# Hash attention and a squared-ReLU MLP on one core: the first pair's query hash products, score halves and first weight piece are put in other places

## The chip, the cores and the metric

The kernel runs on 1 core of one Trainium2 chip, in one launch. The metric is the device time of the kernel in microseconds (us). Before the change the median of 3 runs is 877.55 us (877.53 to 877.87).

## What is computed

Four batches of eight heads with 768 positions of 64 features: queries and keys are hashed to 6 bits by the signs of a projection, attention is allowed only between equal hashes, and the result, (4, 768, 8 x 64) seen as 3072 rows of 512, goes through a two-matrix MLP with a squared ReLU. The weights arrive as 64-bit floats.

```python
q_bucket = np.sum((np.einsum('bhsd,dk->bhsk', q, proj) > 0) * powers, axis=-1)   # k_bucket alike
mask = q_bucket[:, :, :, None] == k_bucket[:, :, None, :]
scores = np.where(mask, scale * np.matmul(q, k.transpose(0, 1, 3, 2)), -1e9)
attn = np.exp(scores - np.max(scores, axis=-1, keepdims=True))
attn = attn / (np.sum(attn, axis=-1, keepdims=True) + 1e-09)
x = np.matmul(attn, v)                     # then (B,H,S,D) -> (B*S, H*D)
r = np.maximum(x @ w_in, 0.0);  out = (r * r) @ w_out
```

## The kernel before, in words

**Stages.** The first stage (to about 330 us of the span) is attention, in a Python loop over 16 pairs of heads, `for pr in range(NP)`. The second is the MLP, with its matrices cut into factors (sums of blocks) so that fewer products are needed; the change does not touch it. Everything is emitted under a manual schedule: each engine executes its instructions in the order in which the code names them.

**One pair.** The two heads of a pair lie on the two halves of the 128 partitions. `feat[pr, w]` holds queries (w = 0) or keys (w = 1) with the features on the partitions. `hash_bits` (matmuls of L346) multiplies them by `projs`; the signs become `bits`, on ScalarE (`signs`, L356) or, for the first pair's keys, on VectorE (`first_keys`, L370 and L374). `score(pr, kt)` makes the scores of one block of 128 keys against all 768 queries: a bf16 product of the bits (the mask) and an fp32 product of the features are added up in one PSUM tile, and ScalarE's exponential (L413) writes them to `e`, one of a ring of four. The 768 queries are cut by `CUTS` into 512 and 256, with one PSUM tile for each cut. `add_up` (L423, L428, VectorE) adds the `e` to `total`; `attend` (L438) multiplies them by the values. Six blocks kt make a pair.

**What one pair leaves to the next.** `finish(pr - 1)`, called within pair pr behind `score(pr, 1)`, issues on TensorE, in this order: the hash products of pair pr + 1 (L346), which need `features(pr + 1)` (two transposes on VectorE, L333); the products `tot` with ones (L455), which need `total`; the last two `attend`; and `spread` (L477), which needs `both`, VectorE's L460, L462 and L466 behind `tot`. `normalize` writes `x_t`.

**PSUM tiles.** `turn()` hands out three tiles in turn, for transposes, hash products, scores and `tot` alike. A matmul that starts a new use waits until the reader of the use three turns before is done.

**The first pair** has its own start: q, k and `projs` are loaded from SP's and ScalarE's queues; TensorE transposes q and k (`first_features`, L309), in two rounds of three blocks of 128 positions each, and ScalarE (L316, q) or VectorE (L318, k) copies them out of PSUM. `keep_busy` (L326) issues matmuls without a use while the loads are under way. The feature products of `score(0, 0)` are issued ahead of its bit products.

**The weights.** They are loaded in 32 pieces of 128 x 512 64-bit floats, two in each pair (a = 2 pr, b = 2 pr + 1), and rounded to fp32 by hand: `part_weight` (VectorE, L143 and L147) splits the exponent from the high word, `place_power` (ScalarE, L160 and L161) moves it to its place, `round_weight` (VectorE, L171, L176, L179) puts sign, mantissa and exponent together and frees the raw piece (one of three buffers), and, for the last piece of each half only, sends DMAs. Piece a is rounded in its own pair and piece b in the next, but for pair 0: there the order of the code is that `place_power(0)` stands behind all six scores and `weigh(1)` (L382, the next pair's keys' bits times their weight), and `round_weight(0)` in pair 1, behind `features(2)`.

Of the kernel before, what the change touches and what calls it, by code (L numbers as in the profile page):

```python
# [34 lines left out]
def kernel(  # L35
# [13 lines left out]
    B, H, S, D = q.shape  # L49
# [5 lines left out]
    HS = S // 2  # L55
# [5 lines left out]
    CUTS = (0, 512), (512, S)  # L61
# [42 lines left out]
    def turn(name):  # L104

        return ps_s.tile([P, 2, 512], FP32, name=name, tag="turn")
# [11 lines left out]
    def goal(i):  # L118
        if i < 2 * NIN:
            return ins[i // NIN][:, i % NIN // 2, i % 2]  # L120
        return p_t.tile([P, DM], FP32, name="out_piece", bufs=3)
# [31 lines left out]
    def place_power(i):  # L153


        if i not in parts:
            return
        power = parts[i][0]
        small = p_w.tile([P, PIECE], U8, name="small")
        nc.scalar.activation(out=small, in_=power, func=ACTF.Relu, bias=excess)  # L160
        nc.scalar.activation(out=power, in_=small, func=ACTF.Copy, scale=2.0**23)  # L161

    def round_weight(i):

        raw = raws.pop(i, None)
        if raw is None:
            return keep_weight(i)
        goals[i] = goal(i)
        low, high = raw[:, :, 0], raw[:, :, 1]
        power, top = parts.pop(i)  # L170
        nc.vector.scalar_tensor_tensor(  # L171
            out=power, in0=high, scalar=0x80000000, in1=power,
            op0=ALU.bitwise_and, op1=ALU.bitwise_or,
        )
        one = top.bitcast(FP32)
        nc.vector.scalar_tensor_tensor(  # L176
            out=one, in0=low, scalar=2.0**-32, in1=top, op0=ALU.mult, op1=ALU.add,
        )
        nc.vector.scalar_tensor_tensor(  # L179
            out=goals[i], in0=one, scalar=2.0**-20, in1=power.bitcast(FP32),  # L180
            op0=ALU.mult, op1=ALU.mult,
        )
        keep_weight(i)

    def keep_weight(i):

        t = goals.pop(i)
        j, c = divmod(i, NIN)
        if j >= 2:
            nc.sync.dma_start(out=w_out_1[:, i - 2 * NIN], in_=t)  # L190
        elif c == NIN - 1:
            nf = NFT // 2
            for n, f, h in (0, 0, 0), (1, nf, 0), (2, nf, 1):
                put_factor(n, j * PIECE, ins[j][:, f:f + nf, h])
            nc.sync.dma_start(
                out=w_in_21[:, :, j * PIECE:(j + 1) * PIECE], in_=ins[j][:, 0:nf, 1]
            )
# [104 lines left out]
    def first_features(w, r):  # L302

        if r == 0:
            feat[0, w] = p_f.tile([P, S], FP32, name=f"feat{w}")
        tp = turn("tp")[:, 0]
        for i in range(SB // 2):
            t = r * (SB // 2) + i
            nc.tensor.transpose(  # L309
                out=tp[:, i * P:(i + 1) * P],  # L310
                in_=nat[0, ("q_nat", "k_nat")[w]][:, t].rearrange("p h d -> p (h d)"),
                identity=ident,
            )
        out = feat[0, w][:, r * HS:(r + 1) * HS]
        if w == 0:
            nc.scalar.copy(out=out, in_=tp[:, 0:HS])  # L316
        else:
            nc.vector.tensor_copy(out=out, in_=tp[:, 0:HS])  # L318

    busy = const.tile([P, 512], BF16, name="busy")  # L320
    void = ps_o.tile([P, 1024], FP32, name="xo")

    def keep_busy(n, w=512):

        for _ in range(n):
            nc.tensor.matmul(  # L326
                out=void[:, 0:w], lhsT=busy[:, 0:P], rhs=busy[:, 0:w], start=True, stop=True
            )
# [8 lines left out]
    def hash_bits(pr, banks, ws=(0, 1), cs=(0, 1)):  # L337


        for w in ws:  # L340
            hashed[pr, w] = banks
            for c in cs:
                g = 2 * w + c
                for h in range(2):
                    rows = slice(h * D, (h + 1) * D)
                    nc.tensor.matmul(  # L346
                        out=banks[g * NR_B:(g + 1) * NR_B, h, 0:HS], lhsT=projs[rows],
                        rhs=feat[pr, w][rows, c * HS:(c + 1) * HS], start=True, stop=True,
                    )

    def signs(pr, w):
        bits[pr, w] = t = all_bits[pr % 2][w]
        for c in range(2):
            at = slice((2 * w + c) * NR_B, (2 * w + c + 1) * NR_B)
            for h in range(2):
                nc.scalar.activation(  # L356
                    out=t[h * D:h * D + NR_B, c * HS:(c + 1) * HS], in_=hashed[pr, w][at, h, 0:HS],
                    func=ACTF.Sign, scale=HUGE, bias=lifts[at],
                )
# [19 lines left out]
    def weigh(pr):  # L379

        t = bits[pr, 1]
        nc.scalar.activation(out=t, in_=t, func=ACTF.Copy, scale=gains)  # L382
# [3 lines left out]
    def score(pr, kt):  # L386

        e = ring[len(weights) % NRING]
        weights[pr, kt] = e
        key = slice(kt * P, (kt + 1) * P)  # L390
        sts = []

        def products(st, lo, hi, src, first):
            for h in range(2):
                rows = slice(h * D, (h + 1) * D)
                nc.tensor.matmul(  # L396
                    out=st[:, h, 0:hi - lo], lhsT=src[pr, 1][rows, key],
                    rhs=src[pr, 0][rows, lo:hi], start=first, stop=not first,
                )


        if (pr, kt) == (0, 0):
            for lo, hi in CUTS:
                sts.append(turn("st"))
                products(sts[-1], lo, hi, feat, True)
        for i, (lo, hi) in enumerate(CUTS):
            if len(sts) <= i:
                sts.append(turn("st"))
                products(sts[i], lo, hi, bits, True)
                products(sts[i], lo, hi, feat, False)  # L410
            else:
                products(sts[i], lo, hi, bits, False)
            nc.scalar.activation(  # L413
                out=e[:, :, lo:hi], in_=sts[i][:, :, 0:hi - lo], func=ACTF.Exp, scale=scale
            )
# [176 lines left out]
    with tc.manual_schedule():  # L592
# [10 lines left out]
        first_features(0, 0)  # L603
        first_features(0, 1)
        keep_busy(2)
        first_features(1, 0)
        hash_bits(0, void.rearrange("p (h c) -> p h c", h=2), (0,))
        signs(0, 0)
        first_keys(0, turn("hash"))
        first_features(1, 1)  # L610
# [3 lines left out]
        for pr in range(NP):  # L614
            a, b = 2 * pr, 2 * pr + 1
            more = pr + 1 < NP

            def prepare():

                hash_bits(pr + 1, turn("hash"))  # L620
                for w in (1, 0):
                    signs(pr + 1, w)


            if pr + 2 < NP:
                load_pair(pr + 2)
            if pr == X_0:
                load_x(0)
            if more and pr > 0:
                for w in range(2):  # L630
                    features(pr + 1, w)
            if pr > 0:
                if pr == 1:
                    round_weight(0)
                round_weight(b - 2)
                load_weight(b)
                for m in sums.get(pr, ()):
                    sum_in(m)
            score(pr, 0)
            if pr == 0:  # L640
                first_keys(1, turn("hash"))
            score(pr, 1)
            if pr == 0:
                for w in range(2):
                    features(1, w)
            if pr > 0:
                finish(pr - 1, prepare if more else None)
            add_up(pr, 1)
            if pr > 0:
                normalize(pr - 1)  # L650


            if pr == X_0 + 1:
                for n in range(2):
                    load_unit(n)
            part_weight(a)
            score(pr, 2)
            if pr == 0:
                prepare()
            score(pr, 3)  # L660
            if more and pr > 0:
                weigh(pr + 1)
            if pr > 0:
                place_power(a)
            attend(pr, 0)
            attend(pr, 1)
            for kt in (2, 3):
                add_up(pr, kt)
            if more:
                load_values(pr + 1)  # L670


            if pr > 0:
                round_weight(a)
            part_weight(b)
            if more:
                load_weight(a + 2)
            score(pr, 4)
            score(pr, 5)
            if pr == 0:  # L680
                weigh(1)
                place_power(0)
            place_power(b)
            attend(pr, 2)
            attend(pr, 3)
            add_up(pr, 4)
            add_up(pr, 5)
# [801 lines left out]
```

## Time and profile before

| what | value |
|---|---|
| median of 3 runs | 877.55 us |
| time of the profiled execution | 877.55 us |
| its span, first to last instruction | 875.8 us |
| what lies around the span | 1.75 us |
| TensorE busy | 864.5 us, 99% of the span |
| VectorE busy | 760.1 us, 87% |
| ScalarE busy | 391.7 us, 45% |
| mean granted TensorE clock | 0.997 |
| idle TensorE, 0 to 7 us / 7 to 12 / 12 to 21 / 21 to 36 | 1.48 / 0.00 / 0.27 / 0.74 us |
| idle TensorE, 36 to 56 / 56 to 320 / 320 to the end | 0.00 / 0.00 / 8.77 us |
| VectorE busy, 36 to 56 / 56 to 320 | 19.59 of 20.00 / 254.27 of 264.00 us |

A row of the timeline gives the start of a group of like instructions on one engine in us from the span's start, the time from its first start to its last end, the engine (PE is TensorE, PEld its weight loads, DVE VectorE, ACT ScalarE, SP and ACTq queues that issue DMAs), the line of the code, the operation, the tiles it writes and reads, the shape, the count, and in brackets how long the engine was idle before it and who ended that. Instructions of one engine overlap at their ends, so the next one can start a tenth of a microsecond before the row's end. An fp32 matmul shows as two records.

### The profile page before, as it was taken

How to read it: one execution, taken by the hardware profiler on the slowest of the kernel's cores; microseconds unless marked ns; L12 is line 12 of the kernel's file. 1: busy time of each engine (PE TensorE's matmuls, PEld its weight loads, DVE VectorE, ACT ScalarE, POOL GpSimd, SP SyncE). 2: the span in 40 equal slices, each digit the busy share in tenths (PEclk: the TensorE clock that was granted, in tenths of full speed). 3: DMA queues.
4: the chain of work that ended last, by engine and by line, in shares of the span. 5: the costliest groups of instructions: out<-in, count | busy, mean ns of one | idle time of the engine just before them, and what ended most of it. 6: DMA issues, size and time to landing. Idle time of an engine off the chain costs nothing.

```text
span 875.8 us, 12135 instructions
## 1 busy us (share of the span) xinstructions
PE 864.5 (99%) x4340; PEld 519.3 (59%) x4340; DVE 760.1 (87%) x1099; ACT 391.7 (45%) x673; POOL 107.1 (12%) x172
## 2 busy tenths in 40 slices
PE   8999999999999999999999999999999999999996
PEld 4444444444444444444688865556888755568885
DVE  5999999999999998888689978888889788888875
ACT  6988788888888852222211123332111233321110
POOL 2000000000000001554032111112000211110002
PEclk9999999999999999999999999999999999999998
DMA  9787967999879526999787874536756754355565
GB/s 176 146 154 134 232 156 150 194 244 234 179 172 226 164 98 223 294 263 288 299 291 259 219 172 156 173 125 219 282 161 177 166 169 152 124 169 158 154 171 109
DMA packets 224131, 167.09 MB, mean 191 GB/s; under 512 B 164448, under 2 KB 181344, under 8 KB 224064
## 3 DMA queue, kind: packets, MB, share of 16 engines
q1 hardware_dynamic: 189152, 87.19, 41.7%
q0 software_dynamic: 12528, 41.30, 15.2%
q10 hardware_dynamic: 22384, 37.76, 14.3%
q8 instruction: 36, 0.59, 0.3%
q14 instruction: 31, 0.25, 0.1%
HBM read 124.52 MB, written 41.68 MB: 190 GB/s over the span
## 4 chain that ended last, share of the span: by engine, by line
PE 95%; DVE 2%; SPq 1%; DMA 1%; issue 0%; ACT 0%; DVEq 0%
PE acc L717 40%; PE st L396 17%; PE acc L936 16%; PE xo L438 13%; PE acc L889 6%; PE hash L346 1%; PE tot L455 1%; DVE total L428 1%; DMA q_nat<-in_q_dram 1%; SPq L287 1%; PE xo L326 0%; PE tp L309 0%; DVE power L171 0%; DVE top L176 0%; DVE feat L333 0%
## 5 line engine op out<-in xcount | busy, mean ns | idle before, releaser
L413 ACT ACTIVATE e<-st 128x1024 f32<-128x1024 f32 x192 | 144.9, 810 | 44.4 <-PE st L396 40.7
L396 PE MATMUL st<-feat,feat 64*128 64x512 f32 (+1 forms) x768 | 150.4, 483 | 0.0
L438 PE MATMUL xo<-e,v_nat 128*64 128x512 f32 (+1 forms) x768 | 134.8, 492 | 0.0
L717 PE MATMUL acc<-b,leaf 128*128 128x256 f32 x600 | 133.1, 379 | 0.0
L717 PEld LDWEIGHTS acc<-b,leaf 128*128 128x128 f32 x600 | 113.8, 190 | 16.2 <-issue 0.9
L428 DVE TENSOR_TENSOR total<-total,e 128x1536 f32<-128x1536 f32 x64 | 112.4, 1756 | 8.1 <-ACT e L413 3.6
L438 PEld LDWEIGHTS xo<-e,v_nat 128*64 128x64 f32 x768 | 51.3, 136 | 82.2 <-issue 74.0
L936 PE MATMUL acc<-t_x,w_unit 128*128 128x512 f32 x192 | 90.2, 592 | 0.0
L396 PEld LDWEIGHTS st<-feat,feat 64*128 64x128 f32 x768 | 66.0, 188 | 32.4 <-issue 22.6
L717 PE MATMUL acc<-t,leaf 128*128 128x256 f32 x336 | 76.2, 380 | 0.0
L356 ACT ACTIVATE bits<-hash,lifts 32x384 bf16<-32x384 f32 x120 | 68.7, 573 | 1.9
L717 PEld LDWEIGHTS acc<-t,leaf 128*128 128x128 f32 x336 | 63.7, 190 | 9.1 <-DVE t L516 0.5
L801 DVE SCALAR_TENSOR_TENSOR b<-h 128x512 f32<-128x512 f32 x96 | 65.7, 692 | 3.0
L396 PE MATMUL st<-bits,bits 64*128 64x256 bf16 (+1 forms) x384 | 63.0, 325 | 0.7 <-ACT bits L356 0.5
L936 PE MATMUL acc<-x,w_unit 128*128 128x512 f32 x128 | 60.1, 592 | 0.0
L717 PE MATMUL acc<-x,w_unit 128*128 128x512 f32 x128 | 56.5, 593 | 0.0
L717 PE MATMUL acc<-b_t,leaf 128*128 128x256 f32 x240 | 53.8, 379 | 0.0
L936 PEld LDWEIGHTS acc<-t_x,w_unit 128*128 128x128 f32 x192 | 36.5, 190 | 28.8 <-issue 26.8
L724 ACT COPY two<-acc 128x256 f32<-128x256 f32 (+1 forms) x29 | 12.5, 432 | 87.7 <-PE acc L717 69.1
L724 ACT COPY one<-acc 128x256 f32<-128x256 f32 (+1 forms) x29 | 12.5, 432 | 84.3 <-PE acc L717 55.5
L717 PEld LDWEIGHTS acc<-b_t,leaf 128*128 128x128 f32 x240 | 45.5, 190 | 6.2
L396 PEld LDWEIGHTS <-bits 64*128 64x128 bf16 x384 | 23.6, 93 | 41.9 <-issue 37.7
(159 smaller groups left out, 1166.5 us busy)
## 6 DMA issues: line engine op xcount, KB each, us to landing
leaf<-w_out ACTq DMA_DIRECT2D x142, 256.0 KB, 3.2
w_unit<-w_in SPq DMA_DIRECT2D x16, 640.0 KB, 4.0
raw<-in_moe_w_in_dram SPq DMA_DIRECT2D x16, 512.0 KB, 5.5
raw<-in_moe_w_out_dram SPq DMA_DIRECT2D x16, 512.0 KB, 4.5
w_unit<-w_in SPq DMA_DIRECT2D x8, 896.0 KB, 7.8
w_out<-sums POOLq DMA_DIRECT2D x16, 448.0 KB, 6.8
sum<-w_in SPq DMA_DIRECT2D x16, 448.0 KB, 4.8
v_nat<-in_v_dram SPq DMA_DIRECT2D x16, 384.0 KB, 4.6
```

The costliest lines, as they stand in the source:

```text
L287: nc.sync.dma_start(out=t[g * 32:(g + 1) * 32].rearrange("i (c d) -> i c d", d=32), in_=src[b, 2 * j + h].rearrange("(c i) (e d) -> e i c ...
L346: nc.tensor.matmul(out=banks[g * NR_B:(g + 1) * NR_B, h, 0:HS], lhsT=projs[rows], rhs=feat[pr, w][rows, c * HS:(c + 1) * HS], start=True, ...
L356: nc.scalar.activation(out=t[h * D:h * D + NR_B, c * HS:(c + 1) * HS], in_=hashed[pr, w][at, h, 0:HS], func=ACTF.Sign, scale=HUGE, bias=li ...
L396: nc.tensor.matmul(out=st[:, h, 0:hi - lo], lhsT=src[pr, 1][rows, key], rhs=src[pr, 0][rows, lo:hi], start=first, stop=not first,)
L413: nc.scalar.activation(out=e[:, :, lo:hi], in_=sts[i][:, :, 0:hi - lo], func=ACTF.Exp, scale=scale)
L428: nc.vector.tensor_tensor(out=totals[pr], in0=totals[pr], in1=weights[pr, kt][:, :, 0:S], op=ALU.add)
L438: nc.tensor.matmul(out=xo[h * D:(h + 1) * D, lo:hi], lhsT=nat[pr, "v_nat"][:, h, kt * D:(kt + 1) * D], rhs=weights[pr, kt][:, h, lo:hi], s ...
L717: nc.tensor.matmul(out=acc[to], lhsT=a(i), rhs=b(i), start=first and i == 0, stop=last and i == n - 1, skip_group_check=True,)
L724: nc.scalar.copy(out=t, in_=acc[of])
L801: nc.vector.scalar_tensor_tensor(out=out, in0=h, scalar=0.0, in1=h, op0=ALU.max, op1=ALU.mult)
L889: nc.tensor.matmul(out=out, lhsT=w[:, a], rhs=b, start=start, stop=stop, skip_group_check=True)
L936: nc.tensor.matmul(out=acc[to], lhsT=w[:, PLACE[a], f], rhs=bt[b](f), start=first and f == 0, stop=last and f == NFT // 2 - 1, skip_group_ ...
```

## The change

Three things are done. (1) In the first pair's start, the queries' hash products stand ahead of the first round of the keys' transposes, and no longer behind it. (2) `score(0, 0)` cuts the 768 queries into 384 and 384; all other blocks keep 512 and 256. (3) In pair 0, `place_power(0)` stands behind `score(0, 3)` and no longer behind `weigh(1)`, and `round_weight(0)` stands in pair 0, behind `add_up(0, 3)` and ahead of `part_weight(1)`, and no longer in pair 1 behind `features(2)`. No arithmetic instruction is added or taken away; the sizes in (2) and the places of the others change.

```diff
+        cuts = CUTS
         if (pr, kt) == (0, 0):
-            for lo, hi in CUTS:
+            cuts = (0, HS), (HS, S)
+            for lo, hi in cuts:
                 sts.append(turn("st"))
                 products(sts[-1], lo, hi, feat, True)
-        for i, (lo, hi) in enumerate(CUTS):
+        for i, (lo, hi) in enumerate(cuts):
...
         keep_busy(2)
+        hash_bits(0, void.rearrange("p (h c) -> p h c", h=2), (0,))
         first_features(1, 0)
-        hash_bits(0, void.rearrange("p (h c) -> p h c", h=2), (0,))
         signs(0, 0)
...
-                if pr == 1:
-                    round_weight(0)
                 round_weight(b - 2)
                 load_weight(b)
...
-            if pr > 0:
-                place_power(a)
+            place_power(a)
...
-            if pr > 0:
-                round_weight(a)
+            round_weight(a)
             part_weight(b)
...
             if pr == 0:
                 weigh(1)
-                place_power(0)
             place_power(b)
```

## The prediction

> **What bounds the kernel now.** First the page: TensorE is the bound, and the chain that ended last runs through it almost alone.
>
> ```profile
> span 875.8 us, 12135 instructions
> PE 864.5 (99%) x4340; PEld 519.3 (59%) x4340; DVE 760.1 (87%) x1099; ACT 391.7 (45%) x673; POOL 107.1 (12%) x172
> ...
> PE 95%; DVE 2%; SPq 1%; DMA 1%; issue 0%; ACT 0%; DVEq 0%
> ```
>
> Then the busy times by stretches: TensorE is idle for 1.48 us before 7 us, 0.27 between 12 and 21, 0.74 between 21 and 36, and not at all from 36 to 320. All of the change lies before 36. So the question is one: when does TensorE leave its last wait of the first two pairs (L477 at 35.73), and so start `score(1, 2)` (35.97)? What comes later follows it one for one, gain or loss.
>
> Then the timeline of the start. To be seen: the keys' way (transposes, copy, hash, signs on VectorE) ends at 10.57 and the queries' signs on ScalarE at 10.67, so the two are level; the bit products follow at 10.74, the first exponential at 11.19.
>
> ```profile
> 1.99 0.57 ACTq L277 DMA_DIRECT2D projs<-in_proj_dram  x1
> 6.39 0.48 ACT L316 COPY feat<-tp 128x384 f32<-128x384 f32 x1 [0.16 <-PE tp L309]
> 6.87 0.55 PE L309 MATMUL tp<-ident,k_nat 128*128 128x128 f32 x3
> 7.35 0.85 PE L346 MATMUL xo<-feat,projs 64*32 64x384 f32 x8
> 7.46 0.56 DVE L318 COPY feat<-tp 128x384 f32<-128x384 f32 x1 [4.17 <-PE tp L309]
> 8.07 0.83 PE L346 MATMUL hash<-feat,projs 64*32 64x384 f32 x4
> 8.84 0.55 PE L309 MATMUL tp<-ident,k_nat 128*128 128x128 f32 x3
> 9.03 1.12 DVE L370 TENSOR_SCALAR bits<-hash 32x384 bf16<-32x384 f32 x2 [1.02 <-PE hash L346]
> 10.21 0.30 PEld L396 LDWEIGHTS st<-feat,feat 64*128 64x128 f32 x4 [0.59 <-DVE bits L370]
> 10.74 0.49 PE L396 MATMUL st<-bits,bits 64*128 64x512 bf16 x4
> 11.19 1.51 ACT L413 ACTIVATE e<-st 128x1024 f32<-128x1024 f32 x2 [0.52 <-PE st L396]
> ```
>
> Then the timeline from the end of the first pair to L477. To be seen: VectorE waits 3.58 us for the exponentials of block 3 and from there has no idle time until `both`, for which TensorE waits.
>
> ```profile
> 21.42 4.50 ACT L413 ACTIVATE e<-st 128x1024 f32<-128x1024 f32 x6
> 22.96 1.76 DVE L428 TENSOR_TENSOR total<-total,e 128x1536 f32<-128x1536 f32 x1 [3.58 <-ACT e L413]
> 26.79 0.71 ACT L160 ACTIVATE small<-power,excess 128x512 uint8<-128x512 uint32 x1
> 29.75 0.93 DVE L333 STREAM_TRANSPOSE feat<-k_nat 128x768 f32<-128x768 f32 x1
> 30.61 0.65 DVE L171 SCALAR_TENSOR_TENSOR power<-raw,power 128x512 uint32<-128x512 uint32 x1
> 31.85 0.85 PE L455 MATMUL tot<-total,ones 128*32 128x384 f32 x8
> 32.63 2.81 PE L438 MATMUL xo<-e,v_nat 128*64 128x512 f32 x16
> 35.73 0.30 PE L477 MATMUL xo<-both,picks 128*64 128x24 f32 x4 [0.29 <-DVE both L466]
> ```
>
> **Step 1, the hash products ahead of the transposes: +1.24 us for the keys.** The queries' hash products cannot start sooner than now: `projs` from ScalarE's queue is issued at 1.99 and, by the table of DMA issues, takes 5.3 us to land, so 7.3, and they start at 7.35. Today the keys' transposes fill that wait. Behind the change they follow: a set of hash products holds TensorE for 0.77 us (8.07 to 8.84), so they start at 8.12 and end, 0.54 later, at 8.66 instead of 7.42. The copy, the hash products and L370 and L374 hang on them one by one, with no spare time between: L370 ends at 11.39 instead of 10.15. The queries' signs gain nothing, and are ready at 10.67 for products that now wait for the keys.
>
> **Step 2, halves: a wait of 0.18 us, then 0.22 us back.** The second half's PSUM tile is the one that L370 reads (third `turn` before). Today that wait is already just met (the row at 10.21). Behind the change the first half's feature products run from 10.55, and the second half's wait for 11.39, start about 11.52 and take 0.71 (768 queries take 1.43, 9.31 to 10.74). The first half's bit products start at 12.23 instead of 10.74 and take about 0.33 (0.38 for 512 columns and 0.27 for 256), so the first exponential starts at 12.62 instead of 11.19: +1.43. By shape the exponentials take 1.026 us for 1024 elements a partition and 0.598 for 512, so 0.81 for 768: the first is 0.22 shorter, and frees the tile for which the next block waits (12.27, 0.21 idle, released by ACT) 1.21 us later than today. From there ScalarE has at most 0.1 us idle between exponentials up to 25.92. So everything up to the exponentials of block 3 is **1.21 us late**. Bounds: 0.85 if `projs` were there when `keep_busy` ends (7.02); 1.43 if the shorter first exponential brings nothing.
>
> **Step 3, the first weight piece in pair 0.** ScalarE: L160 and L161 hold it for 1.27 us (26.79 to 28.06) between blocks 3 and 4, so block 4's first exponential ends 2.48 us late (26.33). The second cut of `score(0, 5)` needs its PSUM tile and had 0.28 us to spare (23.85 to 24.13): it starts at 26.38, +2.25. With what pair 1 now loses at 30.39 (1.24 between cuts, 1.08 elsewhere), which goes, TensorE would reach the hash products of pair 2 2.08 us late, at about 33.12. `weigh(1)` moves behind too and ends at about 29.4, before TensorE needs it (29.77).
> VectorE: L171, L176 and L179 take 1.90 us from start to start (30.61 to 32.51), now ahead of `part_weight(1)`, the last two sums and `features(2)`. Their exponent is there (25.41 against 25.85). So the keys' transpose ends at 30.69 + 1.21 + 1.90 = 33.80, **later than TensorE comes for it** (33.12). The keys' hash products start at 33.85, and `tot` 0.77 later, at 34.62 instead of 31.85: **+2.77**.
> Queues: `round_weight(0)` sends no DMA. It frees its raw buffer sooner, so SP's load of piece 3 (31.89) goes out some 2 us sooner; the piece is not read before 45.35. POOL has no part.
>
> **Step 4, what comes back: -0.56 us.** `both` came late because VectorE had two pieces to round behind `features(2)`; now it has one and is done at about 36.8, before TensorE has ended `attend` (38.2). From `attend` to the next scores is 3.34 us here (32.63 to 35.97), and 2.82 in the next pair, where nothing waits (53.10 to 55.92): 0.52. Another 0.04 is lost today before 39.35, where TensorE waits for `x_t`; 0 to 0.56 are the bounds.
>
> **Sum.** +2.77 - 0.52 - 0.04 = +2.2 us, of which 1.2 is the start. The profiled execution took 877.55 us (span 875.8), which is also the median of the runs, so **879.8 us**, +0.25%. About 0.2% (1.76 us) is what a measurement of this kernel can tell from no change, so "slower" begins at 879.3.
>
> **A rule of the skill against a row.** TensorE stands idle for about 0.65 us behind the keys' transposes (8.66 to 9.31) in the new order. The Trainium skill, "TensorE: Matmul & The Clock Gate", section "A second HAM failure mode: psum-queue depth-cycling", says that short idle times between groups of matmuls can make the clock swing to half. In this trace 0.50 us of idle time at 21.44 leaves the next four 512-column products at 1.03 us, against 1.02 at 42.32 where nothing is idle, and the granted clock is 1.00 on both sides. By the page, an estimate with half clock for one window of 3.4 us adds up to 1.7 us (881.5); by the row nothing. I go by the row.
>
> **Rivals.**
> *A, the start is absorbed; not slower.* If the 1.2 us of the start are taken up before block 3 (by ScalarE's idle 0.85 us at 13.55 and VectorE's 3.58 at 22.96), only 2.77 - 1.21 - 0.56 = +1.0 remains: 878.6. Against it: that 0.85 us is TensorE's answer time to the freed tile, which moves with it, and VectorE's 3.58 is a wait for ScalarE. It decides if block 3's exponentials end before 23.4 (now 22.93).
> *B, VectorE is not late.* If the features are there when TensorE comes, `tot` is 2.08 late: 2.08 - 0.56 = +1.5, 879.1, within the measurement. It needs 0.7 us less on VectorE between 24 and 34; its rows there touch one another already.
> *C, nothing comes back.* If `both` and `x_t` still wait as they do, +2.77; with a first exponential whose half brings nothing as well, +3.0: 880.3 to 880.6. It needs VectorE 1.4 us later at `both` than I have it.
> *D, faster.* A gain over 1.76 us needs more idle time of TensorE than the 1.01 us that lies between 7 and 36 us. Nothing in the profile offers it.
>
> **Chances.** The forecast 0.60; A 0.14; B 0.13; C 0.10; D 0.03. The range takes in A, B and C: 878.5 to 880.8. Slower by over 0.2%: forecast and C, less what of the forecast falls below 879.3 (0.04), 0.66; within 0.2%: 0.31; faster 0.03.
>
> **What would show it.** Right: keys' transposes at about 8.1, first exponential at 12.6, block 3's exponentials ending near 24.1, 1.27 us between blocks 3 and 4 on ScalarE, a wait of TensorE for L333 near 33, none at L477, and then `score(1, 2)` near 38.2 with no idle TensorE to 320. Wrong: the hash products starting before 7.2, `features(2)` ready before 33.1, or the 2.2 us given back behind 36, where I see no idle time to give it.

## The result and the profile after

The changed kernel takes 879.89 us in the median of 6 runs (879.62 to 880.73), the kernel before 877.60 us beside it: a ratio of 1.0027 (95% interval 1.0014 to 1.0040), slower by about 2.3 us. The profiled execution took 879.68 us.

The page after, the lines that answer to those shown of before:

```profile
span 877.9 us, 12130 instructions
PE 865.8 (99%) x4340; PEld 519.7 (59%) x4340; DVE 760.2 (87%) x1099; ACT 391.8 (45%) x673; POOL 107.1 (12%) x172
...
PE 96%; DVE 2%; ACT 1%; issue 0%; DVEq 0%; ACTq 0%
```

The span, first to last instruction, is 2.1 us longer. The chain still runs through TensorE, so the question is the same: when does it start `score(1, 2)`? The view by stretches after (start and end of the stretch and its length, then the busy time of TensorE, its weight loads, VectorE, ScalarE and GpSimd, and the granted clock):

```profile
7.00:12.00 5.00, 4.35 (x27) 1.70 (x28) 2.16 (x5) 2.29 (x4) 0.00 (x0) 1.00 1.32 157
21.00:38.20 17.20, 15.75 (x116) 6.88 (x112) 13.68 (x17) 15.68 (x24) 0.00 (x0) 1.00 0.67 132
38.20:58.00 19.80, 19.80 (x152) 9.02 (x150) 18.54 (x23) 16.81 (x26) 0.00 (x0) 1.00 0.73 134
58.00:322.00 264.00, 264.00 (x1954) 121.66 (x1950) 254.27 (x307) 223.15 (x326) 0.91 (x1) 1.00 0.81 186
```

TensorE is idle for 0.65 us between 7 and 12 (0.00 before) and 1.45 between 21 and 38.2 (0.74 before, to 36), and never from there to 322. The idle time tells only about half of the loss: 1.1 us of 2.28. The rest sits in busy rows that grew without a matmul more. In three of them a later part of the group waits inside the row: pair 2's hash products hold a row of 1.47 us that was 0.88, the queries' first ones 1.03 instead of 0.85, the first feature products 1.81 instead of 1.60. The fourth, the last two matmuls of `keep_busy` (1.06 instead of 0.87), grew because TensorE came to its full rate later in this execution (see the run with `projs` between q and k). So the loss is read from starts, not from the sum of idle times.

The timeline of the start, after (columns as before):

```profile
7.18 1.03 PE L346 MATMUL xo<-feat,projs 64*32 64x384 f32 x8
8.15 0.55 PE L309 MATMUL tp<-ident,k_nat 128*128 128x128 f32 x3
9.35 0.83 PE L346 MATMUL hash<-feat,projs 64*32 64x384 f32 x4 [0.65 <-DVE feat L318]
10.31 1.12 DVE L370 TENSOR_SCALAR bits<-hash 32x384 bf16<-32x384 f32 x2 [1.02 <-PE hash L346]
12.24 0.49 PE L396 MATMUL st<-bits,bits 64*128 64x384 bf16 x4
12.63 1.51 ACT L415 ACTIVATE e<-st 128x768 f32<-128x768 f32 x2 [1.94 <-PE st L396]
13.49 0.39 PE L396 MATMUL st<-bits,bits 64*128 64x512 bf16 x2
```

The keys' transposes moved from 6.87 to 8.15 and the first exponential from 11.19 to 12.63; the next block starts at 13.49 instead of 12.27, 1.22 late.

The timeline from the end of the first pair, after:

```profile
24.17 0.72 ACT L160 ACTIVATE small<-power,excess 128x512 uint8<-128x512 uint32 x1
25.46 2.90 ACT L415 ACTIVATE e<-st 128x1024 f32<-128x1024 f32 x4
25.85 0.68 DVE L171 SCALAR_TENSOR_TENSOR power<-raw,power 128x512 uint32<-128x512 uint32 x1
26.52 0.29 PE L396 MATMUL st<-bits,bits 64*128 64x256 bf16 x2 [0.99 <-ACT e L415]
32.88 0.94 DVE L333 STREAM_TRANSPOSE feat<-k_nat 128x768 f32<-128x768 f32 x1
33.25 1.47 PE L346 MATMUL hash<-feat,projs 64*32 64x384 f32 x16
34.65 0.85 PE L457 MATMUL tot<-total,ones 128*32 128x384 f32 x8
36.70 0.18 DVE L468 TENSOR_TENSOR both<-which,once 128x24 f32<-128x24 f32 x1
38.07 0.26 PE L479 MATMUL xo<-both,picks 128*64 128x24 f32 x4
38.25 0.39 PE L396 MATMUL st<-bits,bits 64*128 64x512 bf16 x2
```

Its last row is the start of `score(1, 2)`. The same row of before:

```profile
35.97 0.39 PE L396 MATMUL st<-bits,bits 64*128 64x512 bf16 x2
```

The exponent (L160 and L161) holds ScalarE from 24.17 to 25.46. The keys' features are ready at 33.81, where TensorE has been since 33.25; `tot` starts at 34.65 instead of 31.85. `both` is ready at 36.88, long before TensorE asks for it at 38.07: the wait of before is gone. `score(1, 2)` starts at 38.25, 2.28 late, the next `attend` 2.24 late, and the last pair's `tot` (328.80 instead of 326.56) 2.24 late: the loss is made in the first 38 us and carried unchanged through 290 us.

### The profile page after: what moved, and what is told of

It reads as the page before. It is cut to its first block, busy times and chain, and to the rows that moved or that the text cites. A ratio compares the mean times of both kernels' runs of the same rounds, so it can differ in the third digit from the quotient of the medians.

```text
span 877.9 us, 12130 instructions
## 1 busy us (share of the span) xinstructions
PE 865.8 (99%) x4340; PEld 519.7 (59%) x4340; DVE 760.2 (87%) x1099; ACT 391.8 (45%) x673; POOL 107.1 (12%) x172
## 4 chain that ended last, share of the span: by engine, by line
PE 96%; DVE 2%; ACT 1%; issue 0%; DVEq 0%; ACTq 0%
PE acc L714 40%; PE st L396 17%; PE acc L933 16%; PE xo L440 14%; PE acc L886 6%; PE hash L346 2%; PE tot L457 1%; DVE total L430 1%; ACT bits L356 1%; PE xo L326 1%; ACT e L415 0%; PE tp L309 0%; PE xo L479 0%; DVE x_t L495 0%; PE xo L346 0%
## 5 line engine op out<-in xcount | busy, mean ns | idle before, releaser
L415 ACT ACTIVATE e<-st 128x1024 f32<-128x1024 f32 (+1 forms) x192 | 145.0, 810 | 46.1 <-PE st L396 42.3
L396 PE MATMUL st<-feat,feat 64*128 64x256 f32 (+2 forms) x768 | 150.6, 484 | 0.0
L396 PEld LDWEIGHTS st<-feat,feat 64*128 64x128 f32 x768 | 66.0, 188 | 33.1 <-issue 23.4
L396 PE MATMUL st<-bits,bits 64*128 64x256 bf16 (+2 forms) x384 | 63.0, 325 | 1.5 <-ACT e L415 1.0
```

What stands on the lines that cost most here:

```text
L396: nc.tensor.matmul(out=st[:, h, 0:hi - lo], lhsT=src[pr, 1][rows, key], rhs=src[pr, 0][rows, lo:hi], start=first, stop=not first,)
L415: nc.scalar.activation(out=e[:, :, lo:hi], in_=sts[i][:, :, 0:hi - lo], func=ACTF.Exp, scale=scale)
```

## The experiments

DMA landings, and the moment at which TensorE comes to its full rate, move the start of the keys' transposes by some tenths of a microsecond from execution to execution (6.5 to 7.0 us where the hash products stand behind them). So times within a profile are compared from that start on where it says "from the transposes", and from the start of `score(0, 1)` (12.27 before) where it says "from the next block". Each edit is against the kernel before unless it says otherwise; "before" is the median beside it: 877.40 us for the three runs of one part alone and `gap_vector`, 877.22 for the other four of the first eight, 877.68 for the three with a strict rotation. The ratio and its interval come from all runs; the quotient of the two medians can differ from the ratio by 0.0002.

### Part 1 alone: the hash products ahead of the transposes

```diff
         keep_busy(2)
+        hash_bits(0, void.rearrange("p (h c) -> p h c", h=2), (0,))
         first_features(1, 0)
-        hash_bits(0, void.rearrange("p (h c) -> p h c", h=2), (0,))
```

> The kernel before with the first part alone: the queries' hash products ahead of the keys' transposes, no halves, weights' piece as before. My theory (the keys' way is late and nothing absorbs it): transposes of the keys at 8.1 us, first exponential at about 12.5 (+1.3), and the scores (1, 2) start at 37.3 instead of 35.97; time 877.6 + 1.3 = 878.9. Rival 'the start is absorbed': block 3's exponentials end by 23.4 and the time stays at 877.6.

878.63 us (+1.23; ratio 1.0012, 1.0003 to 1.0021). The row that matters, in the timeline of this kernel:

```profile
6.96 1.05 PE L346 MATMUL xo<-feat,projs 64*32 64x384 f32 x8 [0.49 <-DMA projs<-in_proj_dram]
```

The hash products wait for the load of `projs`, with the transposes behind them at 7.94 (6.87 before). `score(1, 2)` starts at 37.02, +1.05; `projs` landed 0.21 us sooner in this profile than in the changed kernel's (7.12 against 7.33).

### Part 2 alone: the halves

The hunk on `cuts` of the diff above, alone.

> The kernel before with the second part alone: score (0, 0) in halves of 384. My theory: the wait for the hash products' tile costs about 0.2 us at the first exponential (11.4 instead of 11.19), the shorter exponential gives 0.2 back, so the scores (1, 2) start within 0.1 of 35.97 and the time is 877.6. Rival 'the halves gain by an earlier first exponential': 0.3 to 0.6 us faster, 877.1.

877.16 us (-0.24; ratio 0.9999, 0.9990 to 1.0008). From the transposes, the first exponential is 0.16 late, the next block 0.06 early, `score(1, 2)` 0.06 early. The wait for L370's tile and the shorter first exponential cancel out, as worked out.

### Part 3 alone: the first weight piece in pair 0

The hunks on `place_power` and `round_weight` of the diff above, alone.

> The kernel before with the third part alone: the first weight piece's exponent behind block 3's exponentials, its rounding in pair 0. My theory: VectorE brings the features of pair 2 1.9 us later, TensorE waits for them, and 0.56 comes back behind them: the scores (1, 2) start at 37.0 (+1.0), time 878.6. Rival 'VectorE is not late, only ScalarE's 1.27 us counts': +0.3, 877.9. Rival 'nothing of the start counts, this part carries it all': +2.2, 879.8.

878.58 us (+1.18; ratio 1.0013, 1.0004 to 1.0022). TensorE waits 0.99 us at the second cut of `score(0, 5)`, as in the changed kernel; from the transposes, `tot` is 1.58 late and `score(1, 2)` 1.06: the 0.52 that `both` gives back. The parts add up: 1.23 - 0.24 + 1.18 = 2.2 of the 2.3 us, though the interval of each is some 0.8 us to either side. By the starts of `score(1, 2)`, which tell more, it is 1.05 - 0.06 + 1.06 = 2.05 of 2.28, and the 0.21 us by which `projs` landed sooner in the profile of part 1 accounts for most of the rest.

### Part 1's cause: `projs` loaded between q and k (an edit of the changed kernel)

```diff
             nat[0, name] = t
-        for h, queue in enumerate((nc.sync, nc.scalar)):
-            queue.dma_start(out=projs[h * D:(h + 1) * D, 0:NBITS], in_=proj)
+            if name == "q_nat":
+                for h, queue in enumerate((nc.sync, nc.scalar)):
+                    queue.dma_start(out=projs[h * D:(h + 1) * D, 0:NBITS], in_=proj)
```

> The kernel after, but projs is loaded between q and k and no longer behind k. My theory (the queries' hash products stand in the way of the transposes while they wait for projs, to 7.4): they start when the filler matmuls end (7.0 to 7.1), the transposes of the keys 0.3 sooner if k is there by then (7.8 instead of 8.15), and all that follows is 0.3 sooner: first exponential near 12.3, scores (1, 2) near 37.9; time 0.3 below the kernel after. Rival 'the 0.77 us of the hash products themselves and k's landing set it': no change.

879.14 us (+1.92; ratio 1.0023, 1.0013 to 1.0032). In its timeline:

```profile
4.52 0.82 PE L310 MATMUL tp<-ident,q_nat 128*128 128x128 f32 x6
5.70 1.10 PE L347 MATMUL xo<-feat,projs 64*32 64x384 f32 x8
7.14 0.52 PE L310 MATMUL tp<-ident,k_nat 128*128 128x128 f32 x3 [0.35 <-DMA k_nat<-in_k_dram]
```

`projs` has landed by 5.06 instead of 7.33, and the hash products are over before the keys are there: they fill a wait again. The next block starts at 12.46 instead of 13.49, and `score(1, 2)` comes 1.04 before the changed kernel's, where 0.3 was expected. But not all of that is the loads' doing. The first row shows q's transposes; in the changed kernel they took nearly twice as long:

```profile
4.87 1.49 PE L309 MATMUL tp<-ident,q_nat 128*128 128x128 f32 x6
```

In every profile TensorE works at half its later rate at first: the 512-column matmuls of `keep_busy` start every 0.43 us, later every 0.22. The trace's record of the granted clock begins where the rate doubles, at 4.15 us here and at 7.22 in the changed kernel (ahead of it the view by stretches shows 1.00 without a record). The edit does not set this moment: in six kernels of this case that start with the same instructions it lies between 4.99 and 7.22. At a late moment `keep_busy` ends at 7.0 to 7.2, as in the profiles before and after, and that is the start of the hash products which the expected 0.3 went by. A fairer comparison is the run with early features, two sections on: it has the changed kernel's loads and an early moment (4.56).

```profile
6.99 0.99 PE L346 MATMUL xo<-feat,projs 64*32 64x384 f32 x8 [1.02 <-DMA projs<-in_proj_dram]
```

There TensorE stands idle for 1.02 us, for `projs` alone, and the next block starts at 13.26. So with the full rate early the load is worth 0.80 us of the start (13.26 to 12.46), and less with the full rate late. The keys set what is left: behind `projs` they land later (7.01 against 6.38), and TensorE waits 0.35 us for them. Of the medians, each against its own kernel before, only 0.4 us shows (+1.92 against +2.29), and the intervals overlap: the time alone does not tell this kernel from the changed one.

### Part 3 taken apart: only the exponent early on ScalarE

```diff
-            if pr > 0:
-                place_power(a)
+            place_power(a)
...
                 weigh(1)
-                place_power(0)
```

> The kernel before with half of the third part: the first piece's exponent on ScalarE behind block 3's exponentials, its rounding on VectorE still in pair 1. My theory (VectorE's rounding ahead of features(2) makes most of the third part's 1.0 us): TensorE is 1.0 late at the scores (0, 5) as in the whole third part, but the features are there in time and 'both' comes only 0.3 later: scores (1, 2) at 0.35 later than in the kernel before, time +0.3. Rival 'ScalarE's 1.27 us carry the third part': +1.0, as the whole part.

878.16 us (+0.94; ratio 1.0012, 1.0003 to 1.0021). From the next block, `score(1, 2)` is 0.46 late, near what I expected, but the time is nearer the rival's figure (its interval takes in both). The reason is a wait that neither had, 1.4 us later:

```profile
37.89 0.28 PE L396 MATMUL st<-bits,bits 64*128 64x256 bf16 x2 [0.19 <-ACT bits L356]
```

The second cut of `score(1, 2)` waits for pair 2's signs on ScalarE (they end at 37.84), which began 0.9 late because the exponent had pushed the exponentials ahead of them. From `score(1, 2)` to `attend` is 3.71 us instead of 3.38, and `attend(1, 0)` is 0.8 late. So the exponent alone costs nearly what the whole of part 3 does, but by a wait that the whole of part 3 doesn't have (alone, it has its second cut at 37.81, and the changed kernel at 39.34, both without one). My figure left this wait out.

### Part 3's VectorE half: pair 2's features ahead of the last sum (an edit of the changed kernel)

```diff
-            if more and pr > 0:
+            if more and pr > 1:
...
             add_up(pr, 4)
+            if pr == 0:
+                for w in range(2):
+                    features(2, w)
             add_up(pr, 5)
```

> The kernel after, but features(2) on VectorE stands between the last two sums of pair 0 and no longer behind both. My theory (of the third part's cost, about 0.55 us is TensorE's wait for the features at 33.3 to 33.9): the features are done near 32.1, the hash products of pair 2 run in one go, tot starts at 34.05 instead of 34.65 and the scores (1, 2) at 37.65 instead of 38.25: 0.6 us below the kernel after. Rival 'ScalarE's 1.27 us between blocks 3 and 4 is all, VectorE only looks late': no change against the kernel after, 38.25.

879.57 us (+2.35; ratio 1.0027, 1.0016 to 1.0038). Pair 2's hash products run in one go again, where the changed kernel's row was 1.47 us:

```profile
33.01 0.88 PE L346 MATMUL hash<-feat,projs 64*32 64x384 f32 x16
```

From the transposes, `tot` and `score(1, 2)` start 0.6 earlier than in the changed kernel, as expected: there it was VectorE's features that TensorE waited for. But the same wait for the signs appears (0.19 us at 38.85; `score(1, 2)` to `attend` 3.70 instead of 3.34), and 0.36 us of the gain goes. The remaining 0.24 is too small for the medians, so what the features cost is shown by the starts alone.

### Is a place for the rounding free? Exponent and rounding on VectorE, in its wait

The exponent is done by two VectorE instructions, and these and `round_weight(0)` stand behind (`gap_vector`) or ahead of (`gap2_vector`) the sum of block 2, in the 3.58 us in which VectorE waits for block 3. The diff is that of `gap_vector`; in `gap2_vector` the three lines from `if (pr, kt)` on stand above `add_up(pr, kt)`. In both, `round_weight(0)` in pair 1 goes.

```diff
+    def place_on_vector(i):
+        power = parts[i][0]
+        small = p_w.tile([P, PIECE], U8, name="small")
+        nc.vector.tensor_scalar(
+            out=small, in0=power, scalar1=896.0, scalar2=0.0, op0=ALU.subtract, op1=ALU.max
+        )
+        nc.vector.tensor_scalar(
+            out=power, in0=small, scalar1=2.0**23, scalar2=None, op0=ALU.mult
+        )
...
             for kt in (2, 3):
                 add_up(pr, kt)
+                if (pr, kt) == (0, 2):
+                    place_on_vector(0)
+                    round_weight(0)
...
                 weigh(1)
-                place_power(0)
```

> The kernel before, but the first piece's exponent is placed by VectorE (two instructions of about 0.43 us) and its rounding follows at once, both in the 3.58 us that VectorE waits for block 3's exponentials. My theory (VectorE's order between 24 and 36 us and ScalarE's between blocks 3 and 4 make the cost; both are free in that gap): VectorE's work fits (2.8 of 3.58 us), the wait for 'both' goes (0.5), ScalarE is free 1.3 us sooner (0.2): the scores (1, 2) start at 35.3 instead of 35.97, time 876.9. Rival 'rounding in pair 0 costs wherever it stands': 878.0 or more.

877.19 us (-0.21; ratio 0.9998, 0.9989 to 1.0007).

> As gap_vector (first piece's exponent and rounding on VectorE, in its wait for block 3), but ahead of the sum of block 2 and not behind it. In gap_vector the last sum of pair 0 started 0.42 us later than its data were there, for no reason that I see. If that was chance or the place of the instructions, it goes here and the scores (1, 2) start 0.7 sooner than in the kernel before (35.3 where the keys' transposes start at 6.88); if it belongs to the early rounding, they start 0.43 sooner, as there. Time 0.4 to 0.7 below the kernel before.

876.90 us (-0.32; ratio 0.9998, 0.9989 to 1.0007). Both are within what can be told from no change. Two rows of `gap_vector`'s timeline:

```profile
22.97 1.76 DVE L439 TENSOR_TENSOR total<-total,e 128x1536 f32<-128x1536 f32 x1 [0.75 <-ACT e L424]
27.59 1.76 DVE L439 TENSOR_TENSOR total<-total,e 128x1536 f32<-128x1536 f32 x1 [0.52 <-ACT small L160]
```

All of the piece's VectorE work fits into the wait: 0.75 us of it is left, and the sum of block 3 starts when it did (22.96). So the rounding in pair 0 need not cost anything; part 3 costs because it puts 1.27 us of ScalarE between exponentials that TensorE and VectorE wait for, and 1.90 us of VectorE behind them. From the next block, `score(1, 2)` starts 0.44 and 0.42 us earlier than before, not the 0.7 that I had for the first: the last sum starts 0.4 us late (27.18 before), though its exponentials were done at 25.93. It did so in both kernels, about 0.1 us behind the end of L160 on ScalarE, so neither chance nor the place of the instructions is a likely cause. I have found no dependence that explains it, and no run tells; it stays open.

### The wait for the signs: PSUM tiles in strict rotation

The text ahead of the prediction says that `turn()` hands out three tiles in turn. The waits written into the programs show that this is not strictly so: the pool chooses. In the changed kernel the second cut of `score(1, 2)` waits on TensorE's semaphore and the next block's first cut on ScalarE's; in the kernel before, and in the two that waited for the signs, it is the other way round, the second cut on ScalarE's. That fits a choice between `tot`'s tile and the hash products' tile. These three kernels force the order; the edit is the same in each:

```diff
-    ps_s = first.enter_context(tc.tile_pool(name="ps_s", bufs=3, space=PSUM))
+    ps_s = first.enter_context(tc.tile_pool(name="ps_s", bufs=1, space=PSUM))
+    turns, tiles3 = [], []
     def turn(name):
-        return ps_s.tile([P, 2, 512], FP32, name=name, tag="turn")
+        turns.append(name)
+        i = (len(turns) - 1) % 3
+        if len(turns) <= 3:
+            tiles3.append(ps_s.tile([P, 2, 512], FP32, name=f"turn{i}"))
+        return tiles3[i]
```

> The kernel before, but its three PSUM tiles (scores, transposes, hash products, column sums) are handed out in strict rotation instead of by the pool. In the kernel before, the order of waits has the second cut of score(1,2) wait for ScalarE, that is for the signs of pair 2, 0.11 us before it needs them (36.94 against 37.05); in strict rotation it takes the tile of tot and the next cut takes that of the signs. Theory (only in the early-exponent and early-features kernels does this wait cost anything): no change here, score(1,2) at +0.0, attend(1,0) 3.38 us behind it, time within 0.4 us of the kernel before. Rival (strict rotation brings waits of its own): TensorE has idle time between 36 and 320 us and the time is over 0.5 us longer.

886.50 us (+8.8; ratio 1.0102, 1.0085 to 1.0119). The rival holds, and by far more than it was given. The waits of TensorE in this kernel (total us, times, longest), and one of the 14 in its timeline:

```profile
PE turn L352 <- ACT e L419: 8.3, 14, 0.7
```

```profile
52.40 0.88 PE L352 MATMUL turn<-feat,projs 64*32 64x384 f32 x16 [0.58 <-ACT e L419]
```

In strict rotation each pair's hash products take a tile that an exponential is still reading (it ends at 52.34 here), and wait 0.58 us for it, 14 times. Under the pool's choice the same row has no wait in the kernel before:

```profile
51.51 0.88 PE L346 MATMUL hash<-feat,projs 64*32 64x384 f32 x16
```

> The kernel before with the exponent of piece 0 early on ScalarE (as in the run that did only this), and the three PSUM tiles in strict rotation. Theory: the 0.19 us that TensorE waited at 37.89 for the signs of pair 2 comes from the tile that the pool gave to the second cut of score(1,2); in rotation the cut starts without a wait, attend(1,0) comes 3.34 to 3.38 us behind score(1,2) instead of 3.71, and the time is some 0.35 us below that run: about 877.8 where the kernel before has 877.3. Rival (the scores themselves need something of ScalarE at that point): the wait is there again, 3.71 us, and the time is as in that run (+0.9 against the kernel before).

887.36 us (+9.7; ratio 1.0107, 1.0090 to 1.0124).

> The changed kernel with the features of pair 2 ahead of the last sum of pair 0, and the three PSUM tiles in strict rotation. Theory: the wait of 0.19 us at 38.85 for the signs goes, attend(1,0) comes 3.34 us behind score(1,2) instead of 3.70, so the whole of what the early features give (0.6 us) is kept: time about +1.75 us against the kernel before, instead of the +2.3 of the changed kernel. Rival: the wait is there again and the time stays at +2.3.

888.82 us (+11.1; ratio 1.0127, 1.0110 to 1.0144). The times that I expected of both missed, because the hash products' wait sits on top. The local question is answered: in all three, `score(1, 2)` to `attend(1, 0)` is 3.34 us (36.24 to 39.58, 37.27 to 40.61, 38.43 to 41.77), with no wait for the signs. So that wait came from the tile that the second cut was given, not from what the scores read.

## Why the prediction was right, step by step

The prediction of 879.8 us and its working held; the sum and the times in the table are within 0.15 us.

| step | predicted, us | measured, us |
|---|---|---|
| keys' transposes start | 8.12 | 8.15 |
| L370 ends | 11.39 | 11.43 |
| second half's feature products | 11.52 | 11.49 |
| first exponential starts | 12.62 | 12.63 |
| next block late by | 1.21 | 1.22 |
| second cut of `score(0, 5)` | 26.38 | 26.52 |
| TensorE at pair 2's hash products | 33.12 | 33.25 |
| pair 2's keys' features done | 33.80 | 33.81 |
| `tot` starts | 34.62 | 34.65 |
| `both` done | 36.8 | 36.88 |
| `score(1, 2)` starts | 38.2 | 38.25 |

**Step 1** held, with two of its terms off by about as much in opposite directions. The first hash product started at 7.18 and not at 7.35, because the half of `projs` from SP's queue had landed; the set then held TensorE for 0.97 us and not 0.77, because the other half landed at 7.33. By the letter the start at 7.18 is one of the prediction's signs of being wrong ("before 7.2"), yet the transposes behind it came when it had them. The cause is seen where TensorE stands idle for `projs` (0.49 and 1.02 us in two profiles), and where that load comes sooner: 0.80 us of the start at a like moment of the full rate. The lower bound, 0.85 us "if `projs` were there when `keep_busy` ends (7.02)", took 7.02 for fixed; that end lies between 5.8 and 7.2 us in these profiles, whatever the edit.

**Step 2** held: the first exponential is 1.44 late and the next block 1.22, so 0.22 came back as worked out; alone, the halves move nothing that the time shows.

**Step 3** held, with TensorE 0.13 us later at the hash products than worked out: the exponent and its exponential stand 1.29 us on ScalarE (24.17 to 25.46), and the second cut came 0.14 late. It did not matter, because VectorE was later still, by 0.56 us. The run with early features shows this side of the step by itself.

**Step 4** held to 0.01: `tot` +2.80, `score(1, 2)` +2.28, `attend(1, 0)` +2.24, so 0.52 and 0.04 came back. The run of part 3 alone gives back the same 0.52.

**Rivals.** A fell: block 3's exponentials end at 24.15, beyond its point of decision at 23.4. B fell: the features were 0.56 behind TensorE; the run that moves them shows besides that much of B's gain would have gone to the signs' wait. C fell: `both` has more than a microsecond to spare. D fell. In its step on the queues the prediction named no transfer as late, and none is.

**The rule of the skill against a row.** The row decided. The changed kernel has idle times of 0.65 us (9.35) and 0.99 us (26.52) between TensorE's groups, and its stretches from 7 to 322 us show a granted clock of 1.00, the mean of the whole being 0.998 (0.997 before). The half rate of the first 4 to 7 us lies ahead of any such idle time. The halved clock of the Trainium skill's "TensorE: Matmul & The Clock Gate", section "A second HAM failure mode: psum-queue depth-cycling", follows none of these idle times, nor the 14 waits of 0.58 us in the kernel before with strict rotation (1.00 from 58 to 322 us).

**What stays open**: why the last sum of pair 0 starts 0.4 us late in the two kernels with the exponent on VectorE; and how much of part 1's cost the wait for `projs` makes in the median, since the moment of the full rate is known for the profiled executions only.

## What to carry to other kernels

A small product that waits for a late, tiny load should not stand in front of work whose data are there: order the loads and the products together, or leave the product where it fills a wait. A step moved earlier is worth what its new place has free on every engine it uses; here VectorE had 3.58 us free, and ScalarE none between the exponentials. And when the bound engine shows no idle time behind the edited stretch, find the one instruction from which everything follows and work out its start; sums of idle time show only part of such a delay.

## What the hardware and the pool showed unexpectedly

**Which PSUM tile a matmul is given is worth more than the whole change.** Three tiles in strict rotation cost 8.8 us against the pool's choice, by one wait of 0.58 us in each of 14 pairs; and the pool's choice itself differs between kernels that differ by a few moved instructions, with 0.33 to 0.36 us on it in one pair.

**TensorE comes to its full rate at another moment in each execution.** It does so at 4.15 to 7.22 us in the 13 profiles, at 4.99 to 7.22 in those of the same first instructions, and with it the end of the filler moves. A gain in the first microseconds of one profile can be this and not the edit.

**A load of 1.5 KB takes about as long as the 192 KB queued ahead of it.** `projs`, issued behind q and k on both queues, took 5.2 and 5.3 us from issue to landing in the kernel before (k itself 4.6 and 5.5), and 4.8 to 5.6 in all 12 profiles with that order; between q and k it took 3.2 and 3.6.

**A gain of 0.4 us at `score(1, 2)` can vanish in the time.** `gap_vector` still has 0.48 us in hand at the last pair (its `tot` starts at 326.08 against 326.56), and its last matmul ends later than before's (868.49 against 868.29). From the last `tot` to the last matmul it is 541.7 to 542.4 us in these profiles, so gains of that size are told by the stage's own starts, and not by the time.
